# Transposes of x tile 1 in place of dummy matmuls, the gate row behind block 2, and the attention part last in the last two output tiles of a mixer kernel

## Chip, cores and metric

One core of one Trainium2 chip. The metric is the device time of one launch in microseconds (us). The traced span (first to last instruction) is about 1.7 us shorter than that time.

## The reference

Two mixers share x (2048 x 512); a sigmoid gate, one number for each row, blends them. Cut to what matters:

```python
g = sigmoid((x * gate_w).sum(-1))                  # the gate row
# A: 32-head linear attention with Hedgehog features
o = num / den;  a = o @ wo                         # "attention part"
# B: gated MLP
z = gelu(x @ w_in);  z1, z2 = split(z);  z2 = layernorm(z2)
b = (z1 * (w_sp @ z2 + b_sp)) @ w_out              # "spatial part"
out = g * a + (1 - g) * b
```

## The kernel before

It starts with z2 for tiles 0 and 1 of x (a tile is 128 rows). To have them early they are loaded plainly (`xs`) and transposed on TensorE; tile 2 and later come by transposing DMA. The second z weights (`w_z2`) have four blocks of 128 input rows; the gate row is written in as one more column of them. Dummy matmuls on constants (`warm_up`) keep TensorE busy until data come.

```python
nc.sync.dma_start(out=xs[:, 0, :], in_=x2[0:P, :])
nc.scalar.dma_start(out=w_z2[:, 0, 0:HF], ...)      # block 0, early half
nc.sync.dma_start(out=xs[:, 1, :], in_=x2[P:2 * P, :])
load_z2w(nc.scalar, 1)                              # block 1
load_z2w(nc.sync, 2)                                # block 2
nc.scalar.dma_start(out=w_z2[:, 0, HF:FH], ...)     # block 0, late half
load_z2w(nc.sync, 3)                                # block 3
...
warm_up(6)                        # six dummies, 512 wide
warm_up(2, P)                     # two dummies, 128 wide
x_T(0, 0, 1, ...); x_T(0, 1, NDT, ...)              # transposes of x tile 0
warm_up(3, P)
one(0, 0, 0)                      # one(tile, block, half): z2 matmul
x_T(1, 0, 2, ...); x_T(1, 2, NDT, ..., on_act=True) # transposes of x tile 1
one(0, 1, 0)
warm_up(1, P)
one(1, 0, 0); one(1, 1, 0)
for tt in range(2): z_part(tt, 1, 0, HF, True)      # block 1, late half
gate_T()                          # gate row to a column of w_z2
for tt in range(2): z_part(tt, 0, 0, HF, False)     # block 0, late half
one(0, 2, 0); one(1, 2, 0)        # block 2
...                               # the late half of block 2, then block 3
```

The last two output tiles, one PSUM accumulation each (tile 15 cut into columns 0:384 and 384:512). oT and uT are o and z1 * (w_sp @ z2 + b_sp), transposed by DMA:

```python
def ba_main(acc, tt, c0=0, c1=D):
    oT, uT, i = oTs[tt], uTs[tt], tt % 2
    for g in range(NG):           # attention part: 4 matmuls, needs oT
        nc.tensor.matmul(acc, lhsT=oT[:, g, :], rhs=wo_t[:, g, c0:c1], ...)
    for ft in range(5):           # spatial part: 5 matmuls (+1 in ba_rem), needs uT
        nc.tensor.matmul(acc, lhsT=uT[:, i + ft, :], rhs=w_main[i][:, ft, c0:c1], ...)
...
ba_tile(14)
ba_tile(15, cuts=(0, 384, D))
```

The softmax here doesn't subtract the row's maximum and nothing guards it: scores larger than these inputs give would overflow.

## Time and profile before

| | before |
|---|---|
| time, median of the first 3 runs | 207.75 us (207.62 to 207.82) |
| span of the profiled run (its own time 207.26 us) | 205.5 us |
| TensorE busy | 200.6 us, 98% |

From the page of before, parts 1 and 4: busy time of each engine, and the chain of work that ended last.

```profile
PE 200.6 (98%) x1522; PEld 119.9 (58%) x1540; DVE 128.6 (63%) x276; ACT 75.4 (37%) x123; POOL 45.3 (22%) x73
...
PE 96%; DMA 1%; issue 1%; DVE 0%
```

The waits of TensorE in before (who waited, for whom, us in total, times, longest):

```profile
PE zp L222 <- PEq L594: 0.8, 1, 0.8
PE mm L491 <- DMA oT<-o: 0.4, 1, 0.4
```

TensorE is the limit from end to end. Its list has two waits, the start-up and a wait for oT. The second stands in the TensorE timeline of the last tiles (start us, us, then the group; L491 is the attention part, L493 and L496 the spatial part):

```profile
197.68 1.04 PE L491 MATMUL mm<-wspT,oT 128*128 128x512 bf16 x4
198.55 1.24 PE L493 MATMUL mm<-wspT,uT 128*128 128x512 bf16 x5
199.63 0.38 PE L496 MATMUL mm<-wspT,uT 128*128 128x512 bf16 x1
200.37 0.82 PE L491 MATMUL mm<-wspT,oT 128*128 128x384 bf16 x4 [0.35 <-DMA oT<-o]
201.03 0.98 PE L493 MATMUL mm<-wspT,uT 128*128 128x384 bf16 x5
```

Ends of matmuls overlap the next start, so starts are what to subtract. 512-wide matmuls start 0.216 us apart; after the one at 199.63 the next could have started at 199.85, but started at 200.37: 0.52 us lost.

The TensorE timeline of the head of before (L222 dummies, L284 transposes, L191 and L230 z matmuls, L294 the gate row):

```profile
3.58 0.60 PE L284 MATMUL pq<-ident,xs 128*128 128x128 bf16 x4
4.00 0.34 PE L222 MATMUL zp<-const-bfloat16-1.0 128*128 128x128 bf16 x3
...
5.02 0.47 PE L191 MATMUL zp<-w_z,xT 128*128 128x344 bf16 x2
5.32 0.46 PE L230 MATMUL zp<-w_z,xT 128*128 128x344 bf16 x2
5.62 0.17 PE L294 MATMUL pq<-ident,gaterow 128*128 128x4 bf16 x1
5.68 0.45 PE L230 MATMUL zp<-w_z,xT 128*128 128x344 bf16 x2
5.97 0.60 PE L191 MATMUL zp<-w_z,xT 128*128 128x344 bf16 x3
```

And loads issued around 1.74 us in before, with size and us from issue to landing: block 2 (SP queue), the late half of block 0 (ACT queue), the gate row (POOL queue):

```profile
w_z<-in_B_w_in_dram SPq DMA_DIRECT2D x1, 172.0 KB, 3.7
w_z<-in_B_w_in_dram ACTq DMA_DIRECT2D x1, 86.0 KB, 3.9
gaterow<-in_gate_w_dram POOLq DMA_DIRECT2D x1, 1.0 KB, 3.4
```

### The profile page before, as it was taken

The page shows a single profiled execution, that of the slowest core. Times are in us where ns is not written, and L with a number is a line of the kernel's source. Part 1 is how long each engine was busy: PE and PEld are TensorE (multiplying, and loading weights), DVE is VectorE, ACT ScalarE, POOL GpSimd, SP SyncE. Part 2 cuts the span into 40 slices and gives each one's busy share as a digit, 9 for nine tenths or more (in the row PEclk, how much of TensorE's full clock was granted, in tenths as well). Part 3 has the DMA queues.
Part 4 walks back from the last instruction along what each step waited for, and adds up shares of the span by engine and source line. Part 5 has one row for each costly group of instructions (what it writes and reads, how often), then busy time and mean ns, then how long its engine had stood idle before and what let it go on. Part 6 is the DMA issues. An engine that isn't in the chain of part 4 may idle for free.

```text
span 205.5 us, 3940 instructions
## 1 busy us (share of the span) xinstructions
PE 200.6 (98%) x1522; PEld 119.9 (58%) x1540; DVE 128.6 (63%) x276; ACT 75.4 (37%) x123; POOL 45.3 (22%) x73
## 2 busy tenths in 40 slices
PE   8999999999999999999999999999999999999994
PEld 4666666655665555656565666555455546665632
DVE  4467484838976597979797689555365654533330
ACT  3566677795222333242424132222352116002231
POOL 5020202022423334424242422222203220200000
PEclk9999999999999999999999999999999999999999
DMA  6999599999998027841243228564645756444642
GB/s 190 262 157 191 96 144 278 192 290 217 243 268 191 3 38 219 253 87 38 53 29 63 51 48 151 111 118 77 126 116 112 80 102 171 80 89 89 104 92 77
DMA packets 90099, 27.22 MB, mean 132 GB/s; under 512 B 84224, under 2 KB 90080, under 8 KB 90080
## 3 DMA queue, kind: packets, MB, share of 16 engines
q1 hardware_dynamic: 87312, 24.55, 62.2%
q10 hardware_dynamic: 2736, 2.42, 3.7%
q8 instruction: 12, 0.20, 0.4%
q14 instruction: 7, 0.06, 0.1%
q0 software_dynamic: 32, 0.00, 0.0%
HBM read 4.15 MB, written 2.10 MB: 30 GB/s over the span
## 4 chain that ended last, share of the span: by engine, by line
PE 96%; DMA 1%; issue 1%; DVE 0%
PE mm L454 36%; PE zp L191 18%; PE mm L359 13%; PE mm L493 8%; PE mm L399 7%; PE mm L491 6%; PE at L467 2%; PE kvacc L415 2%; PE zp L222 2%; DMA oT<-o 1%; PE mm L496 1%; PE zp L311 0%; PE zp L230 0%; PE pq L284 0%; PE pq L311 0%
## 5 line engine op out<-in xcount | busy, mean ns | idle before, releaser
L454 PE MATMUL mm<-z2all,wspT 128*128 128x344 bf16 x512 | 79.9, 309 | 0.0
L454 PEld LDWEIGHTS <-wspT 128*128 128x128 bf16 x512 | 49.0, 98 | 25.7 <-issue 0.4
L191 PE MATMUL zp<-w_z,xT 128*128 128x344 bf16 x252 | 38.0, 309 | 0.0
L363 ACT ACTIVATE eq<-mm 128x512 bf16<-128x512 f32 x32 | 17.4, 594 | 51.3 <-POOL eq L376 21.5
L367 DVE TENSOR_REDUCE zs<-eq 128x64 f32<-128x1024 bf16 x16 | 19.5, 1220 | 20.3 <-ACT eq L363 20.3
L191 PEld LDWEIGHTS <-xT 128*128 128x128 bf16 x252 | 24.2, 98 | 12.0 <-DVE xT L290 0.3
L459 DVE SCALAR_TENSOR_TENSOR ucat<-mm,bT,z1all 128x344 bf16<-128x344 f32 x32 | 17.4, 544 | 21.9 <-PE mm L454 21.9
L376 POOL TENSOR_TENSOR eq<-eq,ratio 128x512 bf16<-128x512 bf16 x16 | 16.9, 1055 | 49.9 <-DVE ratio L375 41.8
L363 ACT ACTIVATE ek<-mm 128x512 bf16<-128x512 f32 x32 | 17.3, 601 | 27.1 <-PE mm L359 27.1
L507 ACT ACTIVATE ob<-mm,g_inv 128x512 bf16<-128x512 f32 (+1 forms) x16 | 10.9, 680 | 33.3 <-PE mm L496 28.8
L367 DVE TENSOR_REDUCE zs<-ek 128x64 f32<-128x1024 bf16 x16 | 19.3, 1208 | 2.8 <-ACT ek L363 2.8
L493 PE MATMUL mm<-wspT,uT 128*128 128x512 bf16 (+2 forms) x85 | 20.1, 366 | 0.0
L359 PEld LDWEIGHTS <-xT 128*128 128x128 bf16 x128 | 12.2, 98 | 12.9 <-PE mm L496 0.8
L376 POOL TENSOR_TENSOR ek<-ek,ratio 128x512 bf16<-128x512 bf16 x16 | 16.9, 1056 | 2.1 <-DVE ratio L375 1.5
L359 PE MATMUL mm<-wq_p,xT 128*128 128x512 bf16 x55 | 16.0, 379 | 0.5
L399 PE MATMUL mm<-wv_sb,xT 128*128 128x512 bf16 x64 | 16.4, 379 | 0.0
L491 PE MATMUL mm<-wspT,oT 128*128 128x512 bf16 (+2 forms) x62 | 15.6, 365 | 0.7 <-DMA oT<-o 0.4
L359 PE MATMUL mm<-wk_p,xT 128*128 128x512 bf16 x61 | 16.1, 379 | 0.2
L209 DVE BATCH_NORM_STATS2 bn<-z2all 128x6 f32<-128x344 bf16 x32 | 14.9, 502 | 0.0
L206 ACT ACTIVATE z2all<-zp 128x688 bf16<-128x688 f32 x16 | 11.8, 743 | 7.2 <-PE zp L191 7.1
L264 ACT ACTIVATE z1all<-zp 128x688 bf16<-128x688 f32 x16 | 11.9, 743 | 5.1 <-PE zp L191 4.7
L493 PEld LDWEIGHTS <-uT 128*128 128x128 bf16 x85 | 8.1, 98 | 9.2
(74 smaller groups left out, 142.5 us busy)
## 6 DMA issues: line engine op xcount, KB each, us to landing
out_dram<-ob ACTq DMA_DIRECT2D x15, 128.0 KB, 1.7
wspT<-in_B_w_out_dram SPq DMA_DIRECT2D x2, 640.0 KB, 4.6
w_z<-in_B_w_in_dram SPq DMA_DIRECT2D x2, 344.0 KB, 4.2
wv_sb<-in_A_wqkv_dram SPq DMA_DIRECT2D x2, 256.0 KB, 3.6
wspT<-in_A_wo_dram SPq DMA_DIRECT2D x2, 256.0 KB, 3.8
w_z<-in_B_w_in_dram SPq DMA_DIRECT2D x2, 172.0 KB, 3.8
xs<-in_A_x_dram SPq DMA_DIRECT2D x2, 128.0 KB, 2.5
uT<-ucat SPq DMA_TRANSPOSE x16, 2.8
```

What stands on the lines that cost most here:

```text
L191: nc.tensor.matmul(zp[:, j, 0:n], lhsT=xT[:, dt, tt * P:(tt + 1) * P], rhs=wt[:, dt, j * HF:j * HF + n], start=(dt == first), stop=(dt == ...
L209: nc.vector.bn_stats(out=bn6[:, tt, j, :], in_=z2v[:, j, :])
L264: nc.scalar.activation(out=z1all[:, tt, :].rearrange("p (j n) -> p j n", j=2), in_=zp[:, :, 0:HF], func=AF.Gelu_apprx_tanh,)
L359: nc.tensor.matmul(ps[:, :], lhsT=xT[:, dt, tt * P:(tt + 1) * P], rhs=w[:, dt, :], start=(dt == 0), stop=(dt == NDT - 1))
L363: nc.scalar.activation(out=e[:, :, a, :], in_=ps[:, :].rearrange("p (h f) -> p h f", f=DH), func=AF.Exp, scale=1.0 - 2.0 * a)
L367: nc.vector.tensor_reduce(out=z[:].rearrange("p h a -> p (h a)"), in_=e[:].rearrange("p h a f -> p (h a) f"), axis=AX.X, op=ALU.add,)
L376: nc.gpsimd.tensor_tensor(out=e[:, :, 1, :], in0=e[:, :, 1, :], in1=ratio[:, :, None].to_broadcast([P, H, DH]), op=ALU.mult)
L399: nc.tensor.matmul(v_ps[:, :], lhsT=xT[:, dt, tt * P:(tt + 1) * P], rhs=wv_sb[:, dt, :], start=(dt == 0), stop=(dt == NDT - 1))
L454: nc.tensor.matmul(gp[:, 0:HF], lhsT=wspT[:, st, tt * P:(tt + 1) * P], rhs=z2all[:, st, j * HF:(j + 1) * HF], start=(st == 0), stop=(st == ...
L459: nc.vector.scalar_tensor_tensor(out=ucat[tt % NU][:, c0 + j * HF:c0 + (j + 1) * HF], in0=gp[:, 0:HF], scalar=bT[:, tt:tt + 1], in1=z1all[ ...
L491: nc.tensor.matmul(acc, lhsT=oT[:, g, :], rhs=wo_t[:, g, c0:c1], start=(g == 0), stop=False)
L493: nc.tensor.matmul(acc, lhsT=uT[:, i + ft, :], rhs=w_main[i][:, ft, c0:c1], start=False, stop=False)
```

## The change

Its intent: real transposes take the place of dummies that only filled time, so that x tile 1 is ready when wanted; the gate row gets out of the way of block 2; and the part of the last tiles that waits for oT comes last. No arithmetic is added or removed except four of the six 128-wide dummies.

```diff
@@ -232,24 +232,22 @@
                 rhs=w_z2[:, dt, HF + c0:HF + c1], start=start, stop=False, skip_group_check=True)
 
         warm_up(6)
-        warm_up(2, P)
         x_T(0, 0, 1, pq_tile([P, 1, P], BF16)[:, :, :])
         x_T(0, 1, NDT, pq_tile([P, 3, P], BF16)[:, :, :])
-        warm_up(3, P)
-        one(0, 0, 0)
+        warm_up(2, P)
         x_T(1, 0, 2, tp1[:, :, :])
         x_T(1, 2, NDT, pq_tile([P, 2, P], BF16)[:, :, :], on_act=True)
+        one(0, 0, 0)
         one(0, 1, 0)
-        warm_up(1, P)
+        z_part(0, 1, 0, HF, True)
         one(1, 0, 0)
         one(1, 1, 0)
-        for tt in range(2):
-            z_part(tt, 1, 0, HF, True)
+        z_part(1, 1, 0, HF, True)
+        one(0, 2, 0)
+        one(1, 2, 0)
         gate_T()
         for tt in range(2):
             z_part(tt, 0, 0, HF, False)
-        one(0, 2, 0)
-        one(1, 2, 0)
         for tt in range(2):
             one(tt, 2, 1)
             for dt in range(2):
@@ the last tiles; ba_main split into ba_attn and ba_spat, start and stop flags as arguments (cut) @@
     def ba_tile(tt, cuts=(0, D)):
         for h, (c0, c1) in enumerate(zip(cuts, cuts[1:])):
             acc = acc_tile()[:, 0:c1 - c0]
-            ba_main(acc, tt, c0, c1)
-            ba_rem(acc, tt, slice(0, P), c0, c1)
+            ba_spat(acc, tt, True, c0, c1)
+            ba_rem(acc, tt, slice(0, P), False, c0, c1)
+            ba_attn(acc, tt, False, True, c0, c1)
             ba_store(acc, tt, c0, c1, h > 0)
@@ ba_step (tiles 0 to 13) keeps its order (cut) @@
```

More of the change, by code (lines that the diff above doesn't have):

```diff
@@ L486, in u_T, with ba_attn, ba_spat, ba_rem @@
         return uT
-    def ba_main(acc, tt, c0=0, c1=D):
-        oT, uT, i = oTs[tt], uTs[tt], tt % 2
+    def ba_attn(acc, tt, start, stop, c0=0, c1=D):
         for g in range(NG):
-            nc.tensor.matmul(acc, lhsT=oT[:, g, :], rhs=wo_t[:, g, c0:c1], start=(g == 0), stop=False)
+            nc.tensor.matmul(acc, lhsT=oTs[tt][:, g, :], rhs=wo_t[:, g, c0:c1],
+                             start=start and g == 0, stop=stop and g == NG - 1)
+    def ba_spat(acc, tt, start, c0=0, c1=D):
+        i = tt % 2
         for ft in range(5):
-            nc.tensor.matmul(acc, lhsT=uT[:, i + ft, :], rhs=w_main[i][:, ft, c0:c1], start=False, stop=False)
-    def ba_rem(acc, tt, rows, c0=0, c1=D):
+            nc.tensor.matmul(acc, lhsT=uTs[tt][:, i + ft, :], rhs=w_main[i][:, ft, c0:c1],
+                             start=start and ft == 0, stop=False)
+    def ba_rem(acc, tt, rows, stop, c0=0, c1=D):
         nc.tensor.matmul(
-            acc, lhsT=uTs[tt][rows, 5 * (1 - tt % 2), :], rhs=w_rem[rows, c0:c1], start=False, stop=True)
+            acc, lhsT=uTs[tt][rows, 5 * (1 - tt % 2), :], rhs=w_rem[rows, c0:c1], start=False, stop=stop)
     def ba_store(acc, tt, c0, c1, on_dve):
@@ L523, in ba_step @@
         accs[tt] = acc_tile()
-        ba_main(accs[tt][:, :], tt)
+        ba_attn(accs[tt][:, :], tt, True, False)
+        ba_spat(accs[tt][:, :], tt, False)
         if tt == group[-1]:
             for t in group:
-                ba_rem(accs[t][:, :], t, halves[t % 2])
+                ba_rem(accs[t][:, :], t, halves[t % 2], True)
             for t in group:
```

## The prediction

> **What bounds the kernel.** TensorE. The page gives it 200.6 us busy (98%) of a 205.5 us span at clock 1.000. The chain of waits is 96% TensorE; the table of waits has only two for TensorE: 0.8 us before its first instruction and 0.4 us for the transpose DMA of the last attention tile (oT). The change keeps every real matmul, so only the first 7 us and the last 8 us can move.
>
> **Tail (timeline and chain, 195 to 203 us).** Tile 14 runs ten 512-wide matmuls from 197.68 to 199.85 (0.216 us apart). Tile 15 starts with the attention part, which needs oT, issued at 197.25 and landed 3.07 us later; the next matmul starts at 200.37: 0.52 us of issue time lost (the wait list says 0.4, as it counts the modelled drain as busy). The change puts the six spatial matmuls first: 384 wide, 0.162 us apart, 0.97 us in all, from 199.85 to 200.82. oT is there by 200.32. The new need, uT of tile 15, issued at 195.87, lands 2.8 us later (198.67), over 1 us early. Gain 0.52 us, all on the critical path.
>
> **Head (timeline, DMA landings, 0.8 to 7.2 us).** Dummies run cold: transposes at 3.58 are 0.107 us apart, and by 4.0 128-wide dummies are 0.06 apart. The change drops four of six 128-wide dummies (two cold, two warm: estimated 0.33 us) and fills the wait for VectorE's copy of x tile 1 (weight loads idle 0.28 us until 5.02). x tile 0 landed at 3.2, so its transposes can start 0.21 us sooner, the three copies chain (0.22, 0.36, 0.29 us), and the first matmul of tile 1 moves from 5.02 to about 4.75. Then the loads bind. Block 2 of the second z weights, issued at 1.74, lands 3.7 us later (5.45); it is now wanted at about 5.2, so 0.25 us comes back as a wait. Then the gate row, now later, must be copied (0.17 us) before the 345-wide matmul: about 6.2, against 6.26. Last, x tile 2 comes by transpose DMA at 2.69 + 4.4 = 7.1 us; its first matmul ran at about 7.24. So at most 0.14 us can be gained; I expect 0.08.
>
> The Trainium skill, "TensorE: Matmul & The Clock Gate", Part 1, says about 3.4 us of sustained activity releases the clock, on a free-running window. The trace agrees in size (active from 0.85, fast by 4.0). Transposes in place of dummies keep activity nearly gapless, so I expect release at the same time.
>
> **Sum.** 0.52 + 0.08 = 0.60 us: 207.75 becomes 207.15 us. Range 206.8 to 207.5. Faster by over 2%: 0.01; within 2%: 0.98; slower by over 2%: 0.01.
>
> **What would show it.**
> - Tail right: no TensorE wait for oT; tile 15's spatial matmuls follow tile 14 without a gap.
> - Head right: first matmul of x tile 1 near 4.75; a new gap of 0.2 to 0.3 us before block 2's matmuls, ended by their load; first matmul of x tile 2 at 7.1 to 7.2.
> - Head wrong: x tile 2's matmul well before 7.1, or later than 7.24.
>
> **What would make it wrong.** Loads landing some tenths of a us earlier or later (DMA share is around 1 from 2 to 10 us); a gap in the first 4 us that delays the clock's release (about 0.2 us per 512-wide matmul); a middle phase that waits for a DMA and absorbs the head's gain; a last store, not the matmuls, setting the end.

## The result

207.4 us median of 6 runs (207.19 to 207.71) against 207.9 us of before (6 runs, 207.62 to 208.42). The ratio is 0.9975, interval 0.9959 to 0.9991. Ratios here are the mean time of one kernel's fast runs over that of the other's of the same rounds, so not quite the ratio of the medians.

The profiled runs seem to contradict this: the span of after is 205.6 us, that of before 205.5. The reason is in the two ends. The waits of TensorE in after:

```profile
PE zp L222 <- PEq L598: 0.8, 1, 0.8
PE zp L191 <- DMA w_z<-in_B_w_in_dram: 0.5, 1, 0.5
```

The wait for oT is gone; a wait for a weight load is there instead. The tail of after (L494 and L498 spatial, L488 attention):

```profile
198.29 1.25 PE L494 MATMUL mm<-wspT,uT 128*128 128x512 bf16 x5
199.38 0.38 PE L498 MATMUL mm<-wspT,uT 128*128 128x512 bf16 x1
199.59 1.03 PE L488 MATMUL mm<-wspT,oT 128*128 128x512 bf16 x4
200.46 0.98 PE L494 MATMUL mm<-wspT,uT 128*128 128x384 bf16 x5
201.27 0.33 PE L498 MATMUL mm<-wspT,uT 128*128 128x384 bf16 x1
201.43 0.81 PE L488 MATMUL mm<-wspT,oT 128*128 128x384 bf16 x4
```

No gap: tile 15 starts at 200.46, 0.87 us (four times 0.216) after 199.59, and its attention part at 201.43, after oT's landing at 200.93. From the last matmul of the spatial mix (w_sp @ z2) to the last matmul of all the trace has 7.58 us in before and 7.06 in after: 0.52 us.

The head of after (L282 transposes, L292 the gate row):

```profile
4.31 0.42 PE L282 MATMUL pq<-ident,xs 128*128 128x128 bf16 x2
4.53 0.55 PE L191 MATMUL zp<-w_z,xT 128*128 128x344 bf16 x2
4.91 0.31 PE L230 MATMUL zp<-w_z,xT 128*128 128x344 bf16 x1
5.06 0.46 PE L191 MATMUL zp<-w_z,xT 128*128 128x344 bf16 x2
5.35 0.31 PE L230 MATMUL zp<-w_z,xT 128*128 128x344 bf16 x1
6.12 0.45 PE L191 MATMUL zp<-w_z,xT 128*128 128x344 bf16 x2 [0.46 <-DMA w_z<-in_B_w_in_dram]
6.41 0.17 PE L292 MATMUL pq<-ident,gaterow 128*128 128x4 bf16 x1
6.50 0.45 PE L230 MATMUL zp<-w_z,xT 128*128 128x344 bf16 x2
```

and the same three loads in after:

```profile
w_z<-in_B_w_in_dram SPq DMA_DIRECT2D x1, 172.0 KB, 4.3
w_z<-in_B_w_in_dram ACTq DMA_DIRECT2D x1, 86.0 KB, 4.7
gaterow<-in_gate_w_dram POOLq DMA_DIRECT2D x1, 1.0 KB, 4.1
```

The loads were issued at the same moments but landed 0.6 to 0.8 us later. TensorE had done with blocks 0 and 1 at about 5.5 us and waited for block 2 until 6.12. So in these two profiles the head lost 0.61 us and the tail won 0.52. The end of the head is read here from the start of the first GELU, in before and then in after:

```profile
7.15 2.21 ACT L206 ACTIVATE z2all<-zp 128x688 bf16<-128x688 f32 x3 [1.99 <-PE zp L191]
```

```profile
7.76 2.21 ACT L206 ACTIVATE z2all<-zp 128x688 bf16<-128x688 f32 x3 [2.61 <-PE zp L191]
```

Are the later landings the change's doing, or chance?

**Theory.** The whole gain is the tail's 0.52 us. The head ends when late loads let it, in either order; landings scatter from run to run, and the first profile of before happened to meet early ones. **Rivals.** The new head pays too, and one late-landing profile hides it; or the new head costs time, by delaying the release of TensorE's clock or by its order.

### The profile page after: what moved, and what is told of

It reads as the page before. It is cut to its first block, busy times and chain, and to the rows that moved or that the text cites. A ratio compares the mean times of both kernels' runs of the same rounds, so it can differ in the third digit from the quotient of the medians.

```text
span 205.6 us, 3932 instructions
## 1 busy us (share of the span) xinstructions
PE 200.5 (98%) x1518; PEld 119.8 (58%) x1536; DVE 128.6 (63%) x276; ACT 75.5 (37%) x123; POOL 45.2 (22%) x73
## 4 chain that ended last, share of the span: by engine, by line
PE 95%; DMA 2%; issue 1%; SPq 0%; DVE 0%
PE mm L452 36%; PE zp L191 18%; PE mm L357 13%; PE mm L494 8%; PE mm L397 7%; PE mm L488 7%; DMA w_z<-in_B_w_in_dram 2%; PE at L465 2%; PE kvacc L413 2%; PE mm L498 1%; PE zp L309 0%; PE zp L230 0%; SPq L121 0%; SPq L119 0%; PE pq L309 0%
## 5 line engine op out<-in xcount | busy, mean ns | idle before, releaser
L494 PE MATMUL mm<-wspT,uT 128*128 128x512 bf16 (+2 forms) x85 | 20.1, 367 | 0.0
L488 PE MATMUL mm<-wspT,oT 128*128 128x512 bf16 (+2 forms) x62 | 15.6, 365 | 0.3
L494 PEld LDWEIGHTS <-uT 128*128 128x128 bf16 x85 | 8.1, 98 | 9.4 <-issue 0.2
```

The lines of the kernel that those rows point to most:

```text
L488: nc.tensor.matmul(acc, lhsT=oTs[tt][:, g, :], rhs=wo_t[:, g, c0:c1], start=start and g == 0, stop=stop and g == NG - 1)
L494: nc.tensor.matmul(acc, lhsT=uTs[tt][:, i + ft, :], rhs=w_main[i][:, ft, c0:c1], start=start and ft == 0, stop=False)
```

## Experiments

Every kernel ran in a profiled run and five rounds against before. This table is read from the traces. "Fast from" is the start of the first matmul after which starts are 0.146 us apart for 344 columns (0.056 for 128) and no longer 0.287 (0.107). "Rest" is from the first GELU to the end of the span. In e7_gate_early_2 TensorE waited between 6.25 (slow) and 6.67 (fast), so its release lies somewhere between.

| kernel | block 2 lands | late half of block 0 lands | fast from | first GELU | rest | mean time, us |
|---|---|---|---|---|---|---|
| before | 5.44 | 5.64 | 4.1 | 7.15 | 198.40 | 207.95 (39 runs) |
| e3_before | 5.23 | 5.45 | 4.1 | 7.11 | 198.46 | 207.77 |
| e2_head | 5.63 | 5.97 | 4.8 | 7.30 | 198.39 | 207.90 |
| after | 6.08 | 6.45 | 4.8 | 7.76 | 197.89 | 207.41 (12 runs, with c1) |
| c1_after | 5.29 | 5.71 | 5.2 | 7.54 | 197.90 | (in the line above) |
| e1_tail | 6.27 | 6.63 | 5.7 | 8.14 | 197.87 | 207.50 |
| e4_gate_early | 5.00 | 5.41 | 4.2 | 6.92 | 197.91 | 207.07 |
| e7_gate_early_2 | 6.22 | 6.62 | 6.7 | 8.13 | 197.86 | 207.26 |
| e5_gate_first | 6.02 | 6.49 | 5.8 | 7.71 | 197.86 | 207.39 |
| e6_w0_whole | 5.51 | (with the early half) | 6.5 | 8.29 | 197.93 | 207.71 |
| g1_tile15 | 6.03 | 6.61 | 4.6 | 7.83 | 197.86 | 207.46 |
| h1_no_dummies | 5.54 | 6.05 | 6.7 | 8.05 | 197.86 | 208.03 |
| f1_before_light | not loaded | 4.86 | 5.0 | 7.51 | 197.97 | 207.34 |
| f2_after_light | not loaded | 5.26 | 3.8 | 6.79 | 198.00 | 207.05 |

Single runs of one kernel scatter by about 0.3 us (standard deviation of the 39 runs of before: 0.30), so a mean of six is good to about 0.12 us. Two columns already say much: "rest" is 198.4 to 198.5 us with the old tail and 197.9 to 198.0 with the new one (f1 has the old tail and 197.97, told below), and the first GELU moves between 6.8 and 8.3 us. In these traces the scatter from run to run is made in the first 8 us.

### e1_tail: the tail half alone

```diff
@@ the kernel after, with the head of before put back @@
```

> Only the tail half of the change (last two output tiles with the attention part last), on the head of before. My theory: the tail half is the whole gain, so about 0.5 us less than before (ratio about 0.9975), no TensorE wait for oT, and the time from the first matmul of block 3 of z weights to the end of the span is 198.4 us against 198.9 of before. Rival (head and tail both pay): about 0.5 us here but the whole change then is clearly better than this, by 0.1 to 0.3 us.

Measured: correct, 207.55 us median, ratio 0.9975 (0.9959 to 0.9992), the same as the whole change. The rest is 197.87 us against 198.40. No wait for oT is listed, but one for a load, in the old head:

```profile
PE zp L230 <- DMA w_z<-in_B_w_in_dram: 0.4, 1, 0.4
```

The old head waits for loads as well when they land late (6.63 us here): late landings are not the change's doing. (The text on record speaks of the time from block 3's first matmul: 198.36 us here.) The tail alone gives a ratio equal to the whole. The rival, that the whole is better by 0.1 to 0.3 us, is not seen, but not excluded: the means differ by 0.10 us, with about 0.14 of standard error.

### e2_head: the head half alone

```diff
@@ the kernel before, with the head of after put in @@
```

> Only the head half of the change, on the tail of before. My theory: the loads of z weights bind the head in both orders, so the ratio to before is 1.000 within 0.001; the oT wait of 0.4 us is still there. Rival A (the dummies taken out pay in full): 0.3 us less, ratio 0.9985. Rival B (fewer dummies delay the release of the clock and cost time): ratio above 1.000, with cold matmuls up to 4.7 us as in the profile of after.

Measured: correct, 207.83 us median, ratio 0.9994 (0.9975 to 1.0014). The wait for oT is there, and the rest is 198.39 us, that of before:

```profile
PE mm L489 <- DMA oT<-o: 0.3, 1, 0.3
```

A gain of 0.3 us cannot be excluded by the interval, but nothing is seen of one. Cold matmuls lasted to 4.8 us, without a cost that shows in the time.

### e3_before: the control

```diff
@@ the kernel before, unchanged @@
```

> The kernel before, unchanged, as a control. Ratio 1.000; it shows what timing alone can tell apart. If the early landings of the first profile of before (block 2 at 5.44 us) were luck and those of after (6.08 us) are common, this profile shows block 2 at about 5.9 to 6.1 us, and the first matmul of block 3 later than 6.66 us (7.0 to 7.5). If the change itself delayed the loads, it shows 5.4 to 5.5 us again.

Measured: ratio 0.9993 (0.9975 to 1.0011). Block 2 landed at 5.23 us, early again. So this profile alone did not confirm luck; e1_tail, whose loads and head are those of before and which met 6.27 us, and e4_gate_early, which has the new head and met 5.00 us, did. The control reads like e2_head: timing does not tell the new head from the old.

### e4_gate_early and e7_gate_early_2: the gate row and block 0 ahead of block 2

```diff
         z_part(1, 1, 0, HF, True)
-        one(0, 2, 0)
-        one(1, 2, 0)
         gate_T()
         for tt in range(2):
             z_part(tt, 0, 0, HF, False)
+        one(0, 2, 0)
+        one(1, 2, 0)
```

> The kernel after, but with the gate row and the two matmuls of the late half of block 0 ahead of block 2, as in before. In the profile of after that half block landed at 6.45 us, later than block 2 at 6.08. My theory: in this order TensorE waits for the half block first, and the first matmul of block 3 comes about 0.2 us after that of the kernel after at the same landings; time 0.1 to 0.3 us over the whole change. Rival (order of these six does not matter): the same time as the whole change.

> The same kernel as e4, which came out at 0.9955 where I had expected it slower than the whole change. My theory still: at equal landings its head end is the late half of block 0 plus 1.02 us, 0.0 to 0.2 us later than the whole change, and e4 only met early landings (5.41 us); so here it is the same as or slower than the whole change by up to 0.2 us, and the profile obeys the sum. Rival: it is truly faster, ratio 0.9955 again and below that of the whole change.

Measured: e4 ratio 0.9955 (0.9934 to 0.9975), e7 0.9972 (0.9955 to 0.9988); c1_after, in the rounds of e7, 0.998. The trace obeys the sum: the first GELU comes 1.51 us after the landing of the late half of block 0 in both (5.41 to 6.92; 6.62 to 8.13), and 1.31 us after it in after (6.45 to 7.76), 1.22 in g1_tile15, which has the same head (6.61 to 7.83). So where this load binds, the order of the change is 0.2 to 0.3 us better. The times lean the other way: the 12 runs of this order have a mean of 207.17 us, the 12 of after 207.41, with about 0.15 us of standard error on the difference. The expectation for e4, slower than the whole change, was not met. A possible reason, seen in c1 and f2, is a gap of 0.146 us that the order of the change has when loads are early: the gate row, placed behind block 2, is copied too late for the 345-wide matmul. This stays open.

### c1_after: the whole change once more

```diff
@@ the kernel after, unchanged @@
```

> The kernel after, unchanged, in the same rounds as the next three. Ratio to before 0.997 (0.995 to 0.999). From the six profiles so far, the first matmul of block 3 (head end) should come at the later of: landing of the late half of block 0 plus 0.82 us, landing of block 2 plus 1.19 us, or about 6.35 to 6.65 us set by TensorE; and 198.38 us from there to the end.

Measured: ratio 0.998 (0.996 to 0.9999). The head ended at 7.05 us, where the sum gives at most 6.65. Its loads were early enough (5.71 + 0.82 and 5.29 + 1.19 are both about 6.5), but x tile 1 landed at 4.44 us instead of 4.0, and TensorE was slow until 5.2 us. The TensorE timeline of c1_after:

```profile
4.49 0.39 PE L282 MATMUL tp<-ident,xs 128*128 128x128 bf16 x2 [0.28 <-DMA xs<-in_A_x_dram]
4.67 0.42 PE L282 MATMUL pq<-ident,xs 128*128 128x128 bf16 x2
4.89 0.59 PE L191 MATMUL zp<-w_z,xT 128*128 128x344 bf16 x2
5.32 0.31 PE L230 MATMUL zp<-w_z,xT 128*128 128x344 bf16 x1
...
6.22 0.45 PE L230 MATMUL zp<-w_z,xT 128*128 128x344 bf16 x2
6.65 0.31 PE L191 MATMUL zp<-w_z,xT 128*128 128x345 bf16 x1
```

The two matmuls at 4.89 are 0.28 us apart (the next starts at 5.17). The matmuls at 6.22 and 6.36 should be followed at 6.51; the 345-wide one starts at 6.65: that is the gap of the gate row. So late weights are one limit among three; x tile 1 and the clock are the others. My sum had only one term for TensorE and no spread on it.

### e5_gate_first: only the gate row ahead of block 2

```diff
+        gate_T()
         one(0, 2, 0)
         one(1, 2, 0)
-        gate_T()
```

> The kernel after with only the gate row moved ahead of block 2. In every profile so far the gate row landed 0.1 to 0.6 us before block 2. My theory: it then runs inside the wait for block 2 and the 0.07 us gap for its copy goes: the head end is landing of block 2 plus about 1.03 us or the late half of block 0 plus 0.75 us, a gain of 0.0 to 0.15 us on the whole change. Rival (the gate row behind block 2 is needed, as the change says): TensorE waits for the gate row and loses 0.1 us or more. Timing cannot separate these; the trace can.

Measured: correct, ratio 0.9978 (0.9963 to 0.9993). The gate row landed at 5.58 us and was used at 5.93, as soon as TensorE came to it; block 2 followed at 6.06. The first GELU came 1.22 us after the late half of block 0, against 1.31 in after, and the gap is gone; the head ended at 7.22 us, as the sum has it (6.49 + 0.75 = 7.24). The 0.09 us are not this order's alone: g1_tile15, with the gate row behind block 2, has 1.22 too, because there the late half came 0.58 us behind block 2 (0.37 in after) and the copy fitted into the wait. Placing the gate row behind block 2 is not needed; in time it does not show.

### e6_w0_whole: block 0 in one load, an attempt to beat both

```diff
-    nc.scalar.dma_start(out=w_z2[:, 0, 0:HF], in_=w_in_v[:, 0, FH:FH + HF])
+    load_z2w(nc.scalar, 0)
...
-    nc.scalar.dma_start(out=w_z2[:, 0, HF:FH], in_=w_in_v[:, 0, FH + HF:F])
...
+        for tt in range(2):
+            one(tt, 0, 0)
+            z_part(tt, 0, 0, HF, True)
+            one(tt, 1, 0)
+            z_part(tt, 1, 0, HF, False)
+        gate_T()
+        for tt in range(2):
+            one(tt, 2, 0)
```

> The kernel after with block 0 of the second z weights loaded in one piece, first on its queue, and all eight matmuls of blocks 0 and 1 done before the gate row and block 2. My theory (the late half of block 0, which lands 0.2 to 0.4 us behind block 2, holds the head): the head end is landing of block 2 plus 0.75 us, or about 6.4 us set by TensorE, so 0.1 to 0.4 us less than the whole change; ratio to before about 0.9955. Rival (all loads share one rate, so block 2 just lands later, or block 1 now holds the start): no gain over the whole change.

Measured: correct, ratio 0.9993 (0.998 to 1.0007): its mean is 0.30 us over that of after (about 0.15 of standard error), although the rest is that of after. The head ended at 7.80 us, where the sum gives about 6.4. TensorE waits for x tile 0:

```profile
PE pq L278 <- DMA xs<-in_A_x_dram: 0.4, 1, 0.4
```

x tile 0 landed at 3.88 us, where all thirteen other profiles have 3.20 to 3.46, and block 1 at 4.84 (otherwise 4.18 to 4.65). The matmuls stayed slow until 6.5 us; the first two z matmuls of its timeline (L190, L229) start 0.29 us apart:

```profile
5.08 0.49 PE L190 MATMUL zp<-w_z,xT 128*128 128x344 bf16 x1
5.37 0.49 PE L229 MATMUL zp<-w_z,xT 128*128 128x344 bf16 x1
```

In this profile, then, the larger load at the front went with later landings of x tiles 0 and 1 and of block 1, and the first one wanted is x tile 0. The rival's outcome, no gain, came; the causes that it names did not: block 2 (5.51 us) was not late, and the wait was not for block 1.

### f1_before_light and f2_after_light: the late loads out of the way

```diff
@@ the same in before (f1) and after (f2); wrong result on purpose @@
-    load_z2w(nc.sync, 2)
-    load_z2w(nc.sync, 3)
...
-            rhs=wt[:, dt, j * HF:j * HF + n],
+            rhs=wt[:, dt % 2 if wt is w_z2 else dt, j * HF:j * HF + n],
```

> Wrong result on purpose: the kernel before with blocks 2 and 3 of the second z weights not loaded; its matmuls read blocks 0 and 1 again. With f2 it takes the late loads out of the head. If the loads set the scatter of the head, the timed runs here spread less (standard deviation well under 0.3 us) and the first GELU starts at 7.1 us or a little earlier, as TensorE sets it; ratio to before 0.996 to 1.000. If the clock's release sets it, the spread stays about 0.3 us and cold matmuls (0.29 us apart at 344 wide) are still seen until 4 to 6 us.

> Wrong result on purpose: the kernel after, lightened as f1. If only the loads swallowed the gain of the new head, f2 is faster than f1 by the tail's 0.51 us plus 0.2 to 0.3 us, and its first GELU is 0.2 to 0.3 us earlier at the same release of the clock. Rival (the new head has no gain of its own, or the later release of the clock takes it): f2 is faster than f1 by 0.5 us only.

Measured: results wrong as intended (relative error 0.038); ratios 0.9974 (0.9958 to 0.999) and 0.9966 (0.9948 to 0.9983). Three things follow.

First, the scatter stayed: standard deviations 0.27 and 0.39 us. Late loads do not make it alone. The clock's release differs too (5.0 us in f1, 3.8 in f2).

Second, the new head seems to have a gain of its own when loads do not bind. With an early release in all three (3.8 us in f2, 4.1 in the others), f2 starts the first GELU at 6.79 us, and before and e3_before, in which TensorE waited for a weight load by 0.04 us at most, at 7.15 and 7.11: 0.3 us. The difference of the means, 207.34 and 207.05, is 0.29 us with about 0.19 of standard error. It agrees, and does not prove it. (f2 was to be 0.7 to 0.8 us faster than f1; the tail's part of that fell away, as follows.)

Third, f1 broke the expectation for the tail. It has the old tail, and yet its rest is 197.97 us and no wait for oT is listed. The tail of f1 (L489 attention, L494 spatial):

```profile
199.99 0.38 PE L494 MATMUL mm<-wspT,uT 128*128 128x512 bf16 x1
200.20 0.81 PE L489 MATMUL mm<-wspT,oT 128*128 128x384 bf16 x4
```

The next matmul follows after 0.216 us, because oT was there. The last oT in before, then in f1 (us to landing at the end):

```profile
oT<-o SPq DMA_TRANSPOSE x1, 3.1
```

```profile
oT<-o SPq DMA_TRANSPOSE x1, 2.4
```

The landing took 2.43 to 2.44 us in f1, f2 and e6_w0_whole, and 3.06 to 3.08 us in the eleven other profiles, with nothing between. The one thing found that the three share is one or two loads fewer at the start. This bounds what the tail half is worth: it hides a 3.07 us landing, and with 2.43 us there would be nothing to hide.

The traces show what else differs at that moment. The end of a DMA is told by sixteen signals. In all fourteen profiles at least fifteen of them had come by 2.53 us after the issue of the last oT; in the eleven, the sixteenth came at 3.06 to 3.08. In exactly these eleven, one 8 KB packet of the DMA queue that the page of before lists as "q14 instruction" starts 1.83 to 1.94 us after the issue, while oT is on its way. In f1, f2 and e6 it starts 2.6 to 2.8 us after the issue, when oT has landed. So the late last signal goes with this packet. That the packet causes it, and that the missing loads are what moves the packet, no run tests.

### g1_tile15: only tile 15 with the attention part last

```diff
-            ba_spat(acc, tt, True, c0, c1)
-            ba_rem(acc, tt, slice(0, P), False, c0, c1)
-            ba_attn(acc, tt, False, True, c0, c1)
+            if tt == 15:
+                ... the three lines as they were ...
+            else:
+                ba_attn(acc, tt, True, False, c0, c1)
+                ba_spat(acc, tt, False, c0, c1)
+                ba_rem(acc, tt, slice(0, P), True, c0, c1)
```

> The kernel after, but tile 14 keeps its attention part first; only tile 15 has it last. My theory: tile 14's oT was there long before, so its order pays nothing: from the first GELU to the end of the span 197.9 us as with the whole change (198.4 before), no wait for oT, ratio to before 0.9975. Rival (both tiles are needed): the time from the first GELU to the end is 198.0 to 198.4 us.

Measured: correct, ratio 0.998 (0.9965 to 0.9994), rest 197.86 us, no wait for oT. The order of tile 14 pays nothing; tile 15's is the whole of the tail.

### h1_no_dummies: without the six wide dummies

```diff
-        warm_up(6)
```

> The kernel after without the six 512-wide dummies at the start. My theory (activity releases the clock): TensorE's first work is at 3.4 us, cold until 6.5 to 8.5 us, so the first GELU comes 0.5 to 1.5 us later (8.2 to 9.3 us) and the time is 0.4 to 1.4 us over the whole change. Rival (loads hide all of it, or the clock does not depend on the dummies): the same as the whole change.

Measured: correct, ratio 1.0007 (0.9982 to 1.0033), median 207.73 us, mean 208.03 with two runs at 208.59 and 209.13. That is 0.3 us (medians) to 0.6 us (means) over after, and the widest spread of all (standard deviation 0.68; about 0.3 of standard error on the difference of means). TensorE had its first work at 3.50 us and was slow until 6.7; the first GELU at 8.05 is just under the 8.2 to 9.3. The TensorE wait at its start:

```profile
PE pq L281 <- DMA xs<-in_A_x_dram: 3.5, 1, 3.5
```

So the times lean towards keeping the wide dummies. That the clock waited for the activity is not shown by this one profile: e6_w0_whole and e7_gate_early_2, with the wide dummies, were still slow at 6.23 and 6.25 us. Dropping the four small dummies, with the rest of the new head, does not show in the time (e2_head).

## Why the prediction was right or wrong

The time, 207.4 us, lies in the predicted range (206.8 to 207.5, point 207.15), and within 2% of before, as forecast. The forecast gain was 0.60 us; the medians give 0.5 us. The hit rests on the tail. The head's part, 0.08 us, was small against the range, so the time could not test it, and its steps came otherwise in the profile of after. Point by point:

- **Tail, 0.52 us: right, and exact.** Shown by the trace of after, e1_tail (tail alone, ratio 0.9975) and g1_tile15. The predicted signs came: no wait for oT, tile 15's spatial matmuls behind tile 14 without a gap. That the gain hangs on a 3.07 us landing was not foreseen.
- **Head, 0.08 us: neither shown nor refuted.** By means, the whole change gained 0.55 us (207.95 less 207.41), of which the trace puts 0.52 in the tail; what is left for the head, 0.03, is inside the scatter. e2_head says the same.
- **First matmul of x tile 2 at 7.1 to 7.2: 7.85 in after, 7.63 in c1_after.** "Later than 7.24" is what the prediction itself named as the sign that its head is wrong. The prediction took the landings and the release of the clock as fixed: in after the weights and the release came later, in c1 x tile 1 and the release.
- **"First matmul of x tile 1 near 4.75": 5.06 in after.** TensorE was slow until 4.8 us there; in e4_gate_early, fast from 4.2, it is 4.75.
- **"A wait of 0.2 to 0.3 us for block 2, ended by its load": right in kind, off in size.** By starts, as the prediction counts, it was 0.62 us in after (5.50 to 6.12; the wait list says 0.46), 0.70 in g1_tile15 and none in c1_after. I took one profile's landing, 5.45 us, for a constant; the profiles have 5.0 to 6.3.
- **"At most 0.14 us can be gained", from x tile 2 landing at 7.1: wrong.** That transfer landed as early as the others in each run: at 6.52 in e4_gate_early, whose first GELU is 0.23 us ahead of before's. The step that failed is reading an upper bound from one draw of a scattered quantity. It never bound.
- **"I expect release at the same time": not borne out by the first profiles, and not explained by the change.** Fast from 4.1 us in before and 4.8 in after; but heads of before gave 4.1, 4.1, 5.0 and 5.7, and heads of after 3.8 to 6.7. With this few draws the two cannot be told apart. That activity releases the clock is what the Trainium skill, "TensorE: Matmul & The Clock Gate", Part 1, says; h1_no_dummies, slow for 3.2 us from its first work at 3.50, fits it, but e6 and e7, at work from 0.85 us, were slow nearly as late as h1, so these runs do not show it.

Left open: whether the instruction packet is what delays oT; whether the new head changes the odds of a late release; and whether e4's order is truly 0.24 us better than the change. No version was shown to beat after.

## What to carry to other kernels

In an accumulation whose operands arrive at different times, put the one that arrives last at the end: it costs nothing and hid 0.52 us here, all of it at the very last tile. Before crediting or blaming a change in the first microseconds, look at several profiles: with one and the same head, that of before, the first GELU came between 7.11 and 8.14 us here (e3_before, e1_tail), a wider spread than any reordering was shown to make. Splitting the span at a fixed event, here the first GELU, and comparing the rest shows a gain of half a microsecond in one run where whole times need a dozen.

## What the Trainium skill lacked or had wrong

- "TensorE: Matmul & The Clock Gate", Part 1, puts the change to full speed around 4 us into sustained activity, give or take 500 ns, and notes elsewhere in that part that the window is free-running and run-variable. Here, with first work at 0.85 us, full speed began between 3.8 and 6.5 us in twelve profiles (and between 6.25 and 6.67 in e7_gate_early_2), so 2.9 to 5.7 us into activity that was nearly but not quite gapless. The page's clock rates agree: 344 columns start 0.287 us apart before and 0.146 after.
- "DMA: Bandwidth & Descriptors", section "Latency and other measured facts", gives about 600 ns to the first byte of a DMA from the SP or ACT queue and an HBM access latency of 0.2 us on average and 2 us at high load. It gives no spread for the landing of a load that stands behind others in its queue. Here the same 172 KB load, issued at 1.74 us as third of its queue, took 3.3 to 4.5 us to land.
- No page has this: the last transposing DMA of a 128 x 512 bf16 tile, at the end of the kernel, took 3.06 to 3.08 us to land in eleven profiles, in which an 8 KB packet of the instruction queue started 1.83 to 1.94 us after the issue, and 2.43 to 2.44 in the three in which that packet started after the landing. Fifteen of its sixteen signals had come by 2.53 us in all of them.
